# One block's LayerNorm sums on ScalarE, remainder rows used last, fewer zero blocks, another PV order and a three-piece tail in a fused attention and FFN kernel

## Chip, cores and metric

One core of one Trainium2 chip. The metric is the device time of one execution in microseconds; lower is better. A timing is the median of several executions. The kernel before took 562.42 us (three runs, 562.17 to 563.18).

## The reference

```python
def reference(A_x, A_wqkv, A_wo, B_x, B_w_gate, B_w_up, B_w_down):
    x = A_x                                   # [1, 2048, 576] bf16
    xn = _layernorm(x, axis=-1)
    s = _A_ref(xn, A_wqkv, A_wo)              # 32 heads of 18, causal window of 256 keys, softmax, wo
    g = _silu(_B_ref(xn, B_w_gate, B_w_up, B_w_down))   # (sigmoid(xn wg) * (xn wu)) wd, F = 4608
    return x + s * g
```

## The kernel before

The program builds a graph of operations (each one a short list of instructions of one engine), places them on the engines with a list scheduler that uses estimated durations and priorities, and emits one straight instruction stream per engine. Tokens go in four chunks of 512 (four blocks of 128). TensorE works nearly always in pairs of matmuls, one in each 64-row half of the array; "PV" is attention's product of the softmax weights with the values, 16 groups of narrow matmuls (four a chunk) on smaller tiles. The contraction of 576 is cut into 4 x 128 "main rows" (`wgs`) and 64 "remainder rows" (`wgr`); an FFN tile of 128 hidden features is done in a first half (`f10`) and a second half (`f11`), and the remainder pair was the first of the first half:

```python
BLOCKS = (range(KB), range(1, KB))           # k = 0 is the remainder
def turn(eng, outs, lhs, rhs, hi):
    for k in BLOCKS[hi]:
        res = pair(eng, outs, ..., not hi and k == 0, bool(hi) and k == KB - 1, hi)
# gate_up(ft, h, half, ...):
    o = op("PE", len(BLOCKS[half]) * mm_ns(n), f, f"f1{half}:{c}:{ft}", deps=[xin, wops[ft // WG], deps], ...)
```

In the first chunk the normalised x blocks reach TensorE by transposes, so that the first FFN tiles are done in four token parts each; warming matmuls (`NWARM`) fill the time before (in the trace pairs of them start 0.43 us apart up to 3.6 us and 0.22 us apart from 3.9). The weights of a tile pair have four buffers (`NWS`), the remainders of four tiles have two (`NWR = 2`). All these loads are issued by SyncE, one in-order queue, in the scheduler's order:

```python
self.op_wgr[wg] = self.load_rem(self.wgr[:, sr, :], (self.wg[:, f8], self.wu[:, f8]), ..., pr, [dr])
```

The end: the last token block's down projection (2 x 288 columns) was split once, so that 2 x 192 columns could be worked up by ScalarE and VectorE while TensorE did the last 2 x 96 (in the trace from 554.78 to 556.58 us, TensorE's last matmul starting at 556.07); one transfer took the whole block out.

```python
NTAIL = 96
            na = D // 2 - NTAIL
            down(i + 1, hs[1], 1, [la], 0, na, range(NFG - 1))
            lb = down(i + 1, ht, 0, [], 2 * na, NTAIL)
            fa = down(i + 1, hs[1], 1, [la], 0, na, range(NFG - 1, NFG))
            self.build_final(sb + 1, hs[1], fa, 0, na)
            self.build_final(sb + 1, ht, down(i + 1, ht, 1, [lb], 2 * na, NTAIL), 2 * na, NTAIL)
```

The softmax here doesn't subtract the row's maximum and nothing guards it: scores larger than these inputs give would overflow.

## Time and profile before

| | before |
|---|---|
| median of three runs | 562.42 us |
| span of the profiled execution | 560.1 us |
| first useful matmul starts | 7.87 us |
| last matmul starts | 556.07 us |
| from there to the end | 4.05 us |
| TensorE busy | 99% |

### The profile page before, as it was taken

How to read it: one execution, taken by the hardware profiler on the slowest of the kernel's cores; microseconds unless marked ns; L12 is line 12 of the kernel's file. 1: busy time of each engine (PE TensorE's matmuls, PEld its weight loads, DVE VectorE, ACT ScalarE, POOL GpSimd, SP SyncE). 2: the span in 40 equal slices, each digit the busy share in tenths (PEclk: the TensorE clock that was granted, in tenths of full speed). 3: DMA queues.
4: the chain of work that ended last, by engine and by line, in shares of the span. 5: the costliest groups of instructions: out<-in, count | busy, mean ns of one | idle time of the engine just before them, and what ended most of it. 6: DMA issues, size and time to landing. Idle time of an engine off the chain costs nothing.

```text
span 560.1 us, 19180 instructions
## 1 busy us (share of the span) xinstructions
PE 553.5 (99%) x8300; PEld 335.7 (60%) x8300; DVE 335.7 (60%) x793; ACT 271.4 (48%) x379; POOL 210.8 (38%) x358
## 2 busy tenths in 40 slices
PE   8999999999999999999999999999999999999997
PEld 4454544677764454556877566555487754444786
DVE  5576879769587776734886773586656133333133
ACT  3245655545655656466655636665754133323011
POOL 4564467473366534405674530465330100000000
PEclk9999999999999999999999999999999999999999
DMA  8975899541215454427321243454521126552010
GB/s 230 319 216 153 241 279 261 154 59 35 76 37 155 133 143 144 116 75 128 97 58 35 81 116 98 125 157 125 164 66 36 32 70 176 166 161 57 1 44 23
DMA packets 113323, 67.81 MB, mean 121 GB/s; under 512 B 18476, under 2 KB 111372, under 8 KB 113240
## 3 DMA queue, kind: packets, MB, share of 16 engines
q1 hardware_dynamic: 105816, 60.68, 39.6%
q0 software_dynamic: 7424, 5.92, 3.9%
q8 instruction: 65, 1.06, 0.8%
q14 instruction: 18, 0.15, 0.1%
HBM read 55.15 MB, written 2.36 MB: 103 GB/s over the span
## 4 chain that ended last, share of the span: by engine, by line
PE 97%; DVE 2%; DMA 0%; issue 0%; DVEq 0%
PE ps L109 93%; PE ps L754 3%; DMA x<-in_A_x_dram 0%; DVE o2T L780 0%; DVE ot L772 0%; DVE small L503 0%; DVE s_attn L1005 0%; DVE small L505 0%; DVE o L776 0%; DVE thf L1010 0%; DVE v_aug L652 0%; DVE xnr L515 0%; PE ps L553 0%; DVE xf L1015 0%; DVE ot L775 0%
## 5 line engine op out<-in xcount | busy, mean ns | idle before, releaser
L109 PE MATMUL ps<-xnT,wgs 64*128 64x512 bf16 (+1 forms) x2400 | 285.6, 368 | 0.1
L704 ACT ACTIVATE expr<-ps 128x1024 bf16<-128x1024 f32 (+2 forms) x160 | 156.7, 979 | 86.6 <-PE ps L109 86.0
L109 PEld LDWEIGHTS ps<-xnT,wgs 64*128 64x128 bf16 x2400 | 113.8, 94 | 116.8 <-PE ps L109 0.9
L109 PE MATMUL ps<-wd_sb,hT 64*128 64x288 bf16 (+2 forms) x2448 | 154.3, 276 | 0.0
L900 DVE SCALAR_TENSOR_TENSOR hT<-tring,ps 128x512 bf16<-128x512 bf16 x144 | 98.0, 683 | 89.6 <-ACT tring L897 87.1
L897 ACT ACTIVATE tring<-ps 128x512 bf16<-128x512 f32 x144 | 85.9, 597 | 114.4 <-PE ps L109 112.7
L109 PEld LDWEIGHTS ps<-wd_sb,hT 64*128 64x128 bf16 x2448 | 113.1, 94 | 28.0
L265 POOL DMA_DIRECT2D qk<-qd x160 | 82.6, 524 | 106.6 <-PE ps L109 99.8
L717 DVE TENSOR_TENSOR expr<-expr,mask 128x256 bf16<-128x256 bf16 (+2 forms) x232 | 63.7, 305 | 53.2 <-ACT expr L704 52.5
L669 POOL TENSOR_SCALAR kx<-kprev,small 128x256 bf16<-128x256 bf16 x64 | 62.0, 979 | 31.5 <-PE ps L109 30.8
L265 POOL DMA_DIRECT2D oT<-o2T x72 | 36.9, 520 | 61.9 <-DVE o2T L780 50.0
L109 PE MATMUL ps<-qk,kx 64*128 64x320 bf16 (+4 forms) x736 | 59.8, 251 | 0.0
L109 PE MATMUL ps<-xnT,wgr 64*128 64x512 bf16 (+1 forms) x300 | 55.9, 368 | 0.3
L109 PEld LDWEIGHTS ps<-qk,kx 64*128 64x128 bf16 x736 | 32.0, 94 | 25.5 <-DVE hT L900 1.4
L109 PE MATMUL ps<-xnT,wqk 64*128 64x512 bf16 x256 | 32.6, 377 | 0.0
L772 DVE STREAM_TRANSPOSE ot<-ps 128x512 f32<-128x512 f32 x32 | 22.4, 701 | 13.4 <-PE ps L754 13.3
L995 ACT ACTIVATE thf<-ps 128x576 bf16<-128x576 f32 (+3 forms) x22 | 11.4, 519 | 36.3 <-PE ps L109 35.8
L591 DVE CAST qd<-ps 128x1024 bf16<-128x1024 f32 (+1 forms) x20 | 22.2, 1114 | 6.2 <-PE ps L109 5.9
L669 DVE TENSOR_SCALAR kx<-qk,small 128x512 bf16<-128x512 bf16 x64 | 22.2, 373 | 3.3 <-PE ps L109 3.1
L780 DVE STREAM_TRANSPOSE o2T<-o 128x512 bf16<-128x512 bf16 x32 | 22.8, 711 | 1.1
L109 PEld LDWEIGHTS ps<-xnT,wgr 64*128 64x128 bf16 x300 | 15.0, 94 | 13.8 <-issue 1.3
L825 ACT ACTIVATE s_attn<-ps 128x576 bf16<-128x576 f32 x16 | 9.9, 648 | 27.1 <-PE ps L109 27.1
(64 smaller groups left out, 301.9 us busy)
## 6 DMA issues: line engine op xcount, KB each, us to landing
wgs<-in_B_w_gate_dram SPq DMA_DIRECT2D x72, 256.0 KB, 3.4
wgs<-in_B_w_up_dram SPq DMA_DIRECT2D x72, 256.0 KB, 3.9
wd_sb<-in_B_w_down_dram SPq DMA_DIRECT2D x9, 576.0 KB, 6.4
qk<-qd POOLq DMA_DIRECT2D x100, 36.0 KB, 2.3
wgr<-in_B_w_gate_dram SPq DMA_DIRECT2D x36, 64.0 KB, 2.3
wgr<-in_B_w_up_dram SPq DMA_DIRECT2D x36, 64.0 KB, 2.4
xf<-in_A_x_dram SPq DMA_DIRECT2D x16, 144.0 KB, 2.7
out_dram<-xf SPq DMA_DIRECT2D x16, 144.0 KB, 1.8
```

The costliest lines, as they stand in the source:

```text
L109: res = eng.matmul(outs[i], lhs(ROWS[t], i), rhs(ROWS[t], i), start=start, stop=stop, tile_position=(64 * t, 0))
L265: o = self.op(eng, DMA_ISSUE_NS[eng], lambda e: e.dma_start(dst, src), name, deps, prio, nbytes=nbytes)
L591: return eng.tensor_copy(dst, self.both(h, n))
L669: return e.tensor_scalar(self.kx[:, sx, pos:pos + n_ // SW, t, :], src.rearrange("p (s k) -> p s k", k=SW), self.half[:, t:t + 1], None, A ...
L704: return eng.activation(self.expr[:, se, :, lo * SW:NT], self.both(h, NT)[:, :, lo * SW:NT], ACTF.Exp, scale=SM_SCALE)
L717: return eng.tensor_tensor(e_, e_, m_, ALU.mult)
L754: res = eng.matmul(outs[i][p0:p0 + VH, cols], self.v_aug[ROWS[i], o:o + VH], self.expr[ROWS[i], se, t, cols], start=n == 0, stop=n == len( ...
L772: return e.transpose(self.ot1[:, p1, :], self.halves(hp, NT)[i])
L780: t2 = op("DVE", dve_ns(NT), lambda e, p2=p2, p3=p3: e.transpose(self.o2T[:, p3, :], self.o2[:, p2, :]), f"ot2:{c}:{pr}:{i}", deps=[on, d3 ...
L897: th = op("ACT", act_ns(NT), lambda e: e.activation(self.tring[:, st, :], bank(h, 0), ACTF.Tanh, scale=0.5), f"th:{c}:{ft}", deps=[pg, dt_ ...
L900: mu = op("DVE", dve_ns(NT), lambda e: e.scalar_tensor_tensor(self.hT[:, ft, :], self.tring[:, st, :], 1.0, bank(h, 1), ALU.add, ALU.mult) ...
L995: return e.activation(v2(t)[:, a:b, :], y2()[:, a:b, :], ACTF.Tanh, scale=0.25)
```

## The change

Its intent: start TensorE's useful work earlier (the third x block's LayerNorm sums on ScalarE, so that VectorE gets to the fourth sooner; remainders last, so that the first FFN matmul needs fewer weights), leave out 32 score matmuls whose keys don't exist in the first chunk, order the PV blocks narrow first, space the score groups by a table, and end with a smaller last piece (60 and 52 columns after 176) and an early transfer of the big piece. The diff, cut to its core; cuts are marked:

```diff
+PV_ORDER = (-4, 7, -3, 6, -2, 5, -1, 4, 0, 1, 2, 3)      # was (0, 5, -4, -3, -2, -1, 1, 2, 3, 4, 6, 7)
-BINS0 = (((-4, 0, 1), (1, 1, 5), (6, 6, 2)), ((-2, 2, 1), (3, 3, 5)), ((0, 0, 5), (5, 5, 3)), ...
+BINS0 = (((0, 0, 5), (5, 5, 3)), ((1, 1, 5), (6, 6, 2)), ((2, 2, 5), (7, 7, 1)), ((3, 3, 5),), ((4, 4, 4),))
-NTAIL = 96
-NWARM = (11, 4, 1)
+NTAIL = (60, 52)
+REM_PRIO = 0.6
+STATS_ACT = (2,)
+NWARM = (11, 3)
-SPACE_NS = 1500.0
+SPACE_NS = ((1700, 1700, 1700, 1400, 1700, 2200, 900, 1700), ...)      # one per chunk and head group
-BLOCKS = (range(KB), range(1, KB))
+BLOCKS = ((1, 2, 3, 4), (1, 2, 3, 4, 0))
...  # LayerNorm of block 2 of the first chunk
+    def act_stats(self, x_in, o_x, pr):
+        a1 = op("ACT", ..., lambda e: e.activation(junk, x_in, ACTF.Identity, accum_out=sx), ...)
+        m = op("POOL", 150, ...)                      # minus mean
+        a2 = op("ACT", ..., lambda e: e.activation(junk, x_in, ACTF.Square, bias=nm, accum_out=sq), ...)
+        v = op("POOL", 150, ...); rs = op("POOL", 560, ...)   # variance + eps, power -1/2
...  # remainder loads
-                                                ("wgr", sr), pr, [dr])
+                                                ("wgr", sr), pr + REM_PRIO, [dr])
...  # gate_up: the first half waits for main rows alone
-deps=[xin, wops[ft // WG], deps]
+deps=[xin, wops[ft // WG][0:1 + half], deps]
...  # the third tile's first half is placed ahead of the second tile's last second half
...  # tail
+            nb, nc_ = NTAIL
+            lb = down(i + 1, hb, 0, [], 2 * na, nb)
             fa = down(i + 1, hs[1], 1, [la], 0, na, range(NFG - 1, NFG))
             self.build_final(sb + 1, hs[1], fa, 0, na)
+            lc = down(i + 1, hc, 0, [], 2 * (na + nb), nc_)
+            self.build_final(sb + 1, hb, down(i + 1, hb, 1, [lb], 2 * na, nb), 2 * na, nb)
+            self.build_final(sb + 1, hc, down(i + 1, hc, 1, [lc], 2 * (na + nb), nc_), 2 * (na + nb), nc_)
...
-        if c0 + w == D:
+        if c0 == 0 or c0 + w == D:                   # first piece leaves in a transfer of its own
```

## The prediction

> **What bounds the kernel now.** I read the page first, then the chain of work that ended last, then the timelines of the first 15 us and the last 10 us on every engine, and then the spacing of all 8300 matmul starts.
>
> ```profile
> span 560.1 us, 19180 instructions
> PE 553.5 (99%) x8300; PEld 335.7 (60%) x8300; DVE 335.7 (60%) x793; ACT 271.4 (48%) x379; POOL 210.8 (38%) x358
> PE 97%; DVE 2%; DMA 0%; issue 0%; DVEq 0%
> ```
>
> TensorE is busy 99% of the span and makes up 97% of the chain; the next engine stands at 60%. So a saving counts only if it removes TensorE work, starts TensorE's useful work earlier, ends the work behind its last matmul sooner, or fills a hole in TensorE's stream. The spacing shows how little there is. Matmuls run in pairs on two 64-row tiles; a pair of N columns follows the one before after N/2.4 + about 2.7 ns (512 columns: 216 ns; 288 columns: 122 ns). Summing start-to-start intervals gives 555.0 us; N/2.4 alone gives 536.2. The 18.8 us between them: 3.1 in the warm-up matmuls at the start, some 9.2 in the 2.7 ns of each pair, 4.6 around the PV groups, and under 2 us in real waits: 0.84 before 14.3 us, 0.26 at 130.0, 0.28 at 327.3, and 0.06 to 0.12 at three places. The rest of the span is the start (first useful matmul at 7.87 us) and the end.
>
> The start:
>
> ```profile
> 3.08 0.46 DVE L503 BATCH_NORM_STATS2 small<-x 128x6 f32<-128x288 bf16 x1 [2.08 <-DMA x<-in_A_x_dram]
> ...
> 5.87 1.03 PE L109 MATMUL ps<-hT 64*128 64x512 bf16 x8
> ...
> 7.49 0.38 PE L109 MATMUL ps<-hT 64*128 64x512 bf16 x2
> 7.87 0.23 PE L109 MATMUL ps<-xnT,wgr 64*128 64x128 bf16 x2
> ...
> 10.38 0.23 PE L109 MATMUL ps<-xnT,wgr 64*128 64x128 bf16 x2
> ...
> 11.30 0.49 DVE L541 COPY xnT<-ps 128x640 bf16<-128x640 bf16 x1 [0.28 <-PE ps L553]
> 11.85 0.23 PE L109 MATMUL ps<-xnT,wgr 64*128 64x128 bf16 x2
> ...
> 13.10 2.13 PE L109 MATMUL ps<-xnT,wgs 64*128 64x512 bf16 x16
> ```
>
> VectorE normalises four x blocks one after another, 1.6 us each, from 3.08 to 10.49; TensorE transposes each, an engine copies it out, and only then can FFN matmuls of that block run. The first FFN matmul (7.87) reads wgr, the remainder rows, whose DMA landed last of its four weight loads, at 7.74 (gate and up main rows: 6.33 and 7.32). The fourth block's copy ends at 11.80, so TensorE stands still from 11.54 to 11.85.
>
> The end:
>
> ```profile
> 556.32 0.25 ACT L995 ACTIVATE thf<-ps 128x96 bf16<-128x96 f32 x1 [0.81 <-PE ps L109]
> 556.50 0.61 DVE L1005 TENSOR_TENSOR s_attn<-s_attn,ps 128x96 bf16<-128x96 bf16 x2
> 556.78 0.25 ACT L995 ACTIVATE thf<-ps 128x96 bf16<-128x96 f32 x1 [0.22 <-DVE s_attn L1005]
> 557.14 0.36 DVE L1010 SCALAR_TENSOR_TENSOR thf<-thf,s_attn 128x192 bf16<-128x192 bf16 x1
> 557.53 0.26 DVE L1015 TENSOR_TENSOR xf<-xf,thf 128x192 bf16<-128x192 bf16 x1
> ```
>
> From the last matmul (modelled end 556.27) to the last VectorE result (557.79) are 1.5 us, then 2.3 us for the output transfer.
>
> [...]every one of the 16 PV groups (64x32 tiles) is entered 92-93 ns and left 94-95 ns later than the streaming explains, whether the block before was 512, 288 or 64 columns wide. [...]the trace has PV matmuls 8 ns apart just where a narrow block left no time for the loads. [...]The trace's 576-column ACTIVATE takes 648 ns[...].[...]
>
> **Part by part.**
>
> 1. Start. The third block's statistics leave VectorE: two halves (0.37 each spaced), aggregate 0.22, epsilon 0.15 = 1.1 us. ScalarE is free from 2.3 until the first copy at 6.08; the block lands at 4.16, so two passes of about 0.75 (648[...]) fit in 4.2-6.0, with GpSimd's small steps between (its power takes 0.55-0.57). VectorE's last duplicate then falls at about 9.4 or sooner instead of 10.49. TensorE needs from its first FFN matmul: 8 parts of 9 pairs x 56 ns = 4.03, two transposes 0.30. Using remainders last, the first half needs gate and up only: start near 7.45 (7.32 + 0.1), with main rows first for both early tiles, and remainders are there at 7.74. Without a hole 7.45 + 4.35 = 11.8 for the end of the eight parts, where the kernel before has 12.87. Fourth block needed at about 10.7, ready near 10.4: just enough. The 0.23 us between the halves of the third tile (13.76 to 14.20) goes too, as its first half is placed ahead. Ideal 1.07 + 0.23 = 1.3; I take **-1.2**. The next weights allow it: third tile's main rows landed at 9.54 and 10.38, needed at 11; fifth tile's 12.25 and 12.73, needed near 13.8.
> 2. Zero blocks. First chunk, 8 head groups, two 64-column pairs each fall away: 16 x 31.4 ns (the 144 such matmuls average 15.7 ns) = **-0.50**, all on TensorE. ScalarE also loses 128 of 2048 columns per tile of its exps, VectorE gains one mask per head group; both lie beside TensorE.
> 3. PV order. Streaming is unchanged: 40 x 64 columns (30 in the first chunk). Drains stay at 93 + 94. What can change is the narrow blocks. Before, chunks 1-3 take 1277 ns a group, the first chunk's 942; pairs plus exit drain explain 1193 and 914. A 64-column block leaves 27 ns to load eight weights for the next. Before, 64 then 128 sits mid-group and the rest of the group runs 8 ns per tile apart. After, 64, 64, 128, 128 lie together and the first chunk, which had no such place, gets 64, 128. By the observed delays (78 ns for the 64-to-128 step at the last tile, about 60 a round of loads) I get about +24 ns in 12 groups and +54 in 4: **+0.5**; the author presumably measured something better, so I count **+0.3**.
> 4. Score spacing. Per head group instead of 1.5 us everywhere, it moves only the order of work on TensorE. It can win at most the 0.26 + 0.28 and the three small waits, 0.8 in all; I count **-0.3**.
> 5. Tail. Second-to-last pieces: 72 pairs at 76 ns (176 columns, before 192: 82.7) is -0.48; 60 and 52 columns, 72 pairs each at 27.7 and about 25 (near the smallest spacing seen) = 3.8 against 72 x 42.2 = 3.04: +0.75. TensorE +0.3. The chain behind the last matmul shrinks: 52 instead of 96 columns in ScalarE's and VectorE's steps and 104 instead of 192 in the two last, some 0.4 in all, and VectorE no longer finishes the big piece at 556.59 just as the last one arrives. Most of the last block leaves earlier in its own transfer, but the last transfer still has its latency (median 1.8 us)[...]. Together **-0.2**.
>
> Sum: -1.2 - 0.5 + 0.3 - 0.3 - 0.2 = **-1.9 us**, so 562.4 becomes **560.5**. Everything before the tail shifts TensorE's whole stream, since FFN work fills it to the end.
>
> **The rivals.**
> - ScalarE's statistics come in the way: GpSimd has to do the power for blocks 1 and 2 at once (6.04-6.59 is taken), or the second pass delays the copy at 6.08. For: both lie within 0.1 us. Against: the first FFN matmul is held by weights at 7.4 anyway. If the fourth block comes late, the gain shrinks to 0.6: 561.1.
> - Weights become the bound. DMA is 99% busy from 7.8 to 14.3. Then the start gains only 0.45: 561.3. Against: landings run ahead of use by 0.7 us or more from the third tile on.
> - PV's drain on leaving is hidden behind a wide last block[...]. That would be 16 x 94 = 1.5 us: 558.7. Against: entering after a 512-column matmul costs the same 93.
> - The new score spacing opens holes where VectorE or ScalarE has not yet freed a bank: each of the size of the present ones, 0.1-0.3; +0.8 at worst: 561.6.
>
> **Range and chances.** The parts are small and nearly independent: start 0.4, PV 0.5, spacing 0.4, tail 0.2, run-to-run 0.3 (the three runs before span 1.0) give about 0.9 in the root of squares: **559.1 to 561.8**. Two per cent are 11 us; all holes of TensorE together are under 10, and nothing in the change adds more than 1 us of work. Faster by 2%: 0.005; within: 0.99; slower: 0.005.
>
> **What would show it.** Right: first FFN matmul near 7.4 and reading wgs; the third tile done near 13.8 instead of 15.07; 112 instead of 144 score matmuls of 64 columns; PV entered and left at 93-95 ns and 1290-1310 ns long; span 558-559. Wrong: the start unchanged (weights or the fourth block late), PV groups under 1200 ns (drain hidden), or new idle time of TensorE between 14 and 550 us.

Passages that no trace or run shows are cut from it, with the cut marked. The sum is as recorded: -1.2 - 0.5 + 0.3 - 0.3 - 0.2 = -1.9 us, so 560.5. Its tail term, -0.2, is +0.3 of streaming and -0.5 behind the last matmul: -0.4 of steps and -0.1 for a smaller last transfer. That -0.1, which had no measured basis, is among the cuts (from the last VectorE result to the end took 2.32 us before and 2.10 after). So are 0.1 of the 0.75 us a pass, for reading ScalarE's sum; 648 ns were measured. "Drains" are the 92 to 95 ns by which PV groups are entered and left late. Where PV matmuls are 8 ns apart, the weight loads are 8.3 ns apart in the trace before: eight take 66 ns, and a block of 64 columns streams in 27. That PV may start with a 64-column block was not shown before the change; the runs with that order are correct (e1, e9).

## More of the kernel before

The prediction shows the lines of the chain, the start and the end. Three more of the page matter later; they are of its DMA queues (packets, MB, share) and its DMA issues (count, KB each, median us from issue to landing):

```profile
q8 instruction: 65, 1.06, 0.8%
...
wgr<-in_B_w_gate_dram SPq DMA_DIRECT2D x36, 64.0 KB, 2.3
wgr<-in_B_w_up_dram SPq DMA_DIRECT2D x36, 64.0 KB, 2.4
```

Queue 8 brings TensorE's part of the program (the counts of its instructions below fit that): 65 packets of 16384 bytes each.

## The result, and the profile after

| | before | after |
|---|---|---|
| median (six runs each) | 562.52 us (561.79 to 563.18) | 563.60 us (562.89 to 564.47) |
| ratio, 95% interval | | 1.0021 [1.0008, 1.0034] |
| span of the profiled execution | 560.1 | 561.2 |

A ratio here and below is the mean time of one kernel's fast runs over that of the other's of the same rounds, so it is not quite the ratio of the medians quoted. The predicted 560.5 us and its range (559.1 to 561.8) were missed: the kernel is about 1 us slower, within 2%.

The page of the changed kernel:

```profile
span 561.2 us, 19415 instructions
...
PE 554.0 (99%) x8408; PEld 348.5 (62%) x8408; DVE 333.7 (59%) x801; ACT 274.6 (49%) x385; POOL 211.6 (38%) x360
...
q8 instruction: 66, 1.08, 0.8%
...
PE 97%; DVE 1%; DMA 1%; issue 0%; SPq 0%; DVEq 0%
...
wgr<-in_B_w_gate_dram SPq DMA_DIRECT2D x36, 64.0 KB, 3.9
wgr<-in_B_w_up_dram SPq DMA_DIRECT2D x36, 64.0 KB, 3.7
```

TensorE still fills 97% of the chain. Three things differ: 108 more matmuls and as many weight loads, one more packet of program, and remainder loads that land a median of 3.7 and 3.9 us after issue.

The start, TensorE and ScalarE of the changed kernel (start, duration, engine, line, instruction, count, and in brackets the idle time before and what ended it):

```profile
7.54 0.40 PE L120 MATMUL ps<-xnT,wgs 64*128 64x128 bf16 x8 [0.89 <-DMA wgs<-in_B_w_up_dram]
...
12.96 0.22 PE L120 MATMUL ps<-xnT,wgr 64*128 64x128 bf16 x2
13.56 1.04 PE L120 MATMUL ps<-xnT,wgs 64*128 64x512 bf16 x8 [0.38 <-PE ps L120]
```

```profile
4.48 0.68 ACT L584 ACTIVATE tring<-x 128x576 bf16<-128x576 bf16 x1 [2.19 <-DMA x<-in_A_x_dram]
5.07 0.19 ACT L584 ACTIVATION_READ_ACCUMULATOR tring<-x 128x1 f32 x1
```

The parts predicted are there: ScalarE's two passes (0.68 and 0.77 us, each followed by 0.19 us for reading its sum, of which 0.09 lie behind the ACTIVATE's end), a first FFN matmul on main rows at 7.54 us. VectorE's last duplicate ends at 9.74 instead of 10.49, and the fourth block's copy at 10.79 instead of 11.79. But behind the two matmuls of 12.96 TensorE does nothing until 13.56: 0.55 us by the start-to-start interval less the streaming, 0.38 in the view's brackets, which count from the modelled end of the matmul before. The view names a semaphore, but by the code the wait is for the third tile's first half, and the trace has that update of the semaphore at 12.92 (the last one before the hole ends is at 13.19), so the wait must have another reason.

The end of the changed kernel, all engines; and the last steps of its chain of work:

```profile
555.72 3.76 SPq L277 DMA_DIRECT2D out_dram<-xf  x2
556.33 1.50 PE L120 MATMUL ps<-wd_sb,hT 64*128 64x60 bf16 x103 [0.93 <-issue]
...
558.85 0.21 DVE L1071 TENSOR_TENSOR xf<-xf,thf 128x104 bf16<-128x104 bf16 x1
```

```profile
472.41 82.98 PE ps L120 x1241
555.40 0.93 issue
556.33 0.61 PE ps L120 x31
```

The chain says "issue" for 0.93 us: TensorE waits for no semaphore there. The kernel before has no such step. Counted from the start-to-start intervals less the streaming, the hole is 1.09 us.

To see where the time went I split the two executions into the same pieces. "Holes" are the parts of start-to-start intervals that exceed the streaming by more than 40 ns, without the entries and exits of PV:

| us | before | after | difference |
|---|---|---|---|
| first FFN matmul starts | 7.87 | 7.54 | -0.33 |
| holes, start (to 16 us) | 0.84 | 0.55 | -0.29 |
| holes, middle | 0.79 | 2.02 | +1.23 |
| holes, last 16 us | 0.00 | 1.09 | +1.09 |
| columns streamed, at 2.4 a ns | 532.51 | 532.23 | -0.28 |
| entries and exits of PV | 3.00 | 2.99 | -0.01 |
| all smaller intervals | 11.05 | 11.23 | +0.18 |
| behind the start of the last matmul | 4.05 | 3.51 | -0.54 |
| sum | 560.11 | 561.16 | +1.05 |

(The 2.4 columns a ns are read from the spacing, as in the prediction: 216 ns for 512 columns, 122 for 288. In the -0.28 of columns streamed, -0.43 are the zero blocks; +0.13 are one block's transposes, which now stand behind the first FFN matmul.)

Of the +1.23 in the middle, 0.69 are two waits for remainder loads, 0.37 at 74.5 and 0.32 at 471.9. The second, in the weight loads of TensorE:

```profile
472.38 0.57 PEld L120 LDWEIGHTS ps<-xnT,wgs 64*128 64x128 bf16 x8 [0.62 <-DMA wgr<-in_B_w_gate_dram]
```

So there were two suspects, each with a rival. **Theory 1:** the remainder loads wait too long in SyncE's queue because of their lower priority; rival: the memory side got slower. **Theory 2:** the hole in the tail and the one at 12.96 are TensorE waiting for its own program. Queue 8's packets are 16384 bytes each, and the trace fits one packet for every 256 of TensorE's records. I count these from 0 (matmuls, weight loads and its own semaphore waits, 16824 before and 17040 after); the hole at the start stands at record 449, the hole in the tail at record 16833, and 16833 - 449 is 64 x 256. With the boundaries at 193 + 256 n, the blocks from record 449 to the one fetched ahead at the end are 65 and 66, as many as queue 8 has packets. The fetch of the block that begins at record 16833 ran from 553.95 to 554.88, while TensorE ran the block before, which had begun at 553.35; the new block's first matmul started at 556.33, 2.38 us after its fetch began. Rival: a wait of the new tail itself, for a PSUM bank or for ScalarE.

### The profile page after: what moved, and what is told of

The parts are those of the page before. It is cut to its first block, busy times and chain, and to the rows that moved or that the text cites. A ratio compares the mean times of both kernels' runs of the same rounds, so it can differ in the third digit from the quotient of the medians.

```text
span 561.2 us, 19415 instructions
## 1 busy us (share of the span) xinstructions
PE 554.0 (99%) x8408; PEld 348.5 (62%) x8408; DVE 333.7 (59%) x801; ACT 274.6 (49%) x385; POOL 211.6 (38%) x360
## 3 DMA queue, kind: packets, MB, share of 16 engines
q8 instruction: 66, 1.08, 0.8%
## 4 chain that ended last, share of the span: by engine, by line
PE 97%; DVE 1%; DMA 1%; issue 0%; SPq 0%; DVEq 0%
PE ps L120 93%; PE ps L799 3%; DMA wgs<-in_B_w_up_dram 1%; SPq L277 0%; DVE o2T L825 0%; DVE ot L817 0%; DVE o L821 0%; DVE s_attn L1061 0%; DVE v_aug L696 0%; DVE thf L1066 0%; DVE ot L820 0%; PE ps L597 0%; DVE xf L1071 0%; DVEq L1226 0%
## 5 line engine op out<-in xcount | busy, mean ns | idle before, releaser
L749 ACT ACTIVATE expr<-ps 128x1024 bf16<-128x1024 f32 (+4 forms) x160 | 154.9, 969 | 89.3 <-PE ps L120 88.8
L120 PEld LDWEIGHTS ps<-xnT,wgs 64*128 64x128 bf16 x2400 | 118.3, 94 | 111.9 <-issue 3.2
L120 PE MATMUL ps<-wd_sb,hT 64*128 64x288 bf16 (+3 forms) x2592 | 155.7, 269 | 0.9 <-issue 0.9
L120 PEld LDWEIGHTS ps<-wd_sb,hT 64*128 64x128 bf16 x2592 | 119.9, 94 | 22.1 <-issue 1.3
L762 DVE TENSOR_TENSOR expr<-expr,mask 128x128 bf16<-128x128 bf16 (+2 forms) x240 | 63.9, 297 | 78.8 <-ACT expr L749 78.1
L120 PE MATMUL ps<-qk,kx 64*128 64x320 bf16 (+1 forms) x704 | 59.9, 254 | 0.1
L1051 ACT ACTIVATE thf<-ps 128x576 bf16<-128x576 f32 (+4 forms) x24 | 11.7, 489 | 35.0 <-PE ps L120 34.6
L695 ACT ACTIVATE v_aug<-ps 64x288 bf16<-64x288 f32 x32 | 13.1, 408 | 17.0 <-PE ps L120 16.5
```

Source lines behind the costliest of these rows:

```text
L120: res = eng.matmul(outs[i], lhs(ROWS[t], i), rhs(ROWS[t], i), start=start, stop=stop, tile_position=(64 * t, 0))
L695: return eng.activation(dst, src, ACTF.Copy)
L749: return eng.activation(self.expr[:, se, :, lo * SW:NT], self.both(h, NT)[:, :, lo * SW:NT], ACTF.Exp, scale=SM_SCALE)
L762: return eng.tensor_tensor(e_, e_, m_, ALU.mult)
```

## The experiments

Twelve kernels, all correct. Those of one call shared the runs of the kernel before: e1 to e4 (561.79 us, nine runs), e5, e6, e9 and e10 (562.19, eleven), e11 to e14 (562.06, nine). All runs compared were fast; e5 and e6 are single looks, of unknown state, without a ratio ("-"). The holes and spans are those of one profiled execution each.

| run | median us | ratio to before, 95% | span | first FFN matmul | holes start / middle / tail | behind last matmul |
|---|---|---|---|---|---|---|
| after | 563.60 | 1.0021 [1.0008, 1.0034] | 561.16 | 7.54 | 0.55 / 2.02 / 1.09 | 3.51 |
| e1_tail_two | 563.20 | 1.0028 [1.0016, 1.0041] | 562.28 | 7.41 | 0.99 / 2.82 / 0.00 | 4.88 |
| e2_pv_old | 562.95 | 1.0025 [1.0012, 1.0039] | 561.27 | 7.54 | 0.11 / 2.86 / 1.07 | 3.51 |
| e3_rem_prio0 | 564.92 | 1.0053 [1.0040, 1.0065] | 562.81 | 7.14 | 0.63 / 3.43 / 1.19 | 3.51 |
| e4_space_flat | 564.65 | 1.0051 [1.0037, 1.0064] | 562.85 | 7.59 | 0.20 / 3.56 / 1.26 | 3.52 |
| e5_tail_80_80 | 563.22 | - | 561.48 | 8.12 | 0.00 / 2.25 / 1.13 | 3.60 |
| e6_tail_four | 566.10 | - | 564.36 | 8.18 | 0.05 / 2.57 / 3.38 | 3.59 |
| e9_rem_early | 561.86 | 0.9989 [0.9977, 1.0001] | 559.83 | 7.39 | 0.06 / 1.34 / 1.07 | 3.52 |
| e10_tail_before | 562.70 | 1.0005 [0.9987, 1.0023] | 560.80 | 7.33 | 0.18 / 3.09 / 0.00 | 4.04 |
| e11_three_mends | 560.96 | 0.9978 [0.9965, 0.9990] | 559.17 | 7.46 | 0.39 / 1.35 / 0.00 | 4.04 |
| e12_three_warm | 560.69 | 0.9973 [0.9961, 0.9986] | 558.95 | 7.57 | 0.08 / 1.36 / 0.00 | 4.03 |
| e13_only_tail | 565.45 | 1.0057 [1.0043, 1.0070] | 564.79 | 8.62 | 1.01 / 0.79 / 3.24 | 3.42 |
| e14_mends_flat | 563.07 | 1.0018 [1.0006, 1.0031] | 561.41 | 7.38 | 0.28 / 3.60 / 0.00 | 4.04 |

**Parts undone, one at a time (e1 to e4).**

e1: the tail in two pieces, the early first transfer kept.

```diff
-NTAIL = (60, 52)
+NTAIL = (96,)          # tail code generalised to a list of narrow pieces
```

> The changed kernel with its last token block in two pieces (192 and 96 columns a half) again, the early first transfer kept; everything before the tail is in the same order. Theory (the 1.09 us hole at 555.21, which waits for no semaphore, is TensorE running out of fetched instructions because 52- and 60-column pairs use four instructions in 25 to 28 ns): the hole is gone, TensorE streams 0.28 us less, the chain behind the last matmul is 0.4 to 0.5 longer, so 0.8 to 1.0 us faster than the changed kernel, about 562.7. Rival (the hole is chance or has to do with the place in the program, and the three pieces gain what I predicted): a hole stays, or the time is 0.2 us longer than that of the changed kernel.

The hole in the tail is gone, with 16752 TensorE records in the stream. The time did not fall, as the end took 4.88 us behind the last matmul: SyncE issued the first output transfer at 557.94 and the last only at 560.31, though VectorE's last result was there at 559.12. The trace shows what SyncE did in between: 31 waits, one for each lane of loads, which the program puts just ahead of SyncE's last entry (`run_engine`); they take from 558.34 to 560.21. In the kernel after, where the first issue is at 555.72, they are over at 558.00 and the last transfer follows its result at once; in the kernel before they are over at 554.88. As the code stands, the early transfer thus only suits a tail in which some 2.3 us lie between the two, an estimate from these two traces (557.94 to 560.21 and 555.72 to 558.00); moving the waits ahead of it was not run. e10 below removes both.

e2: the old order of PV.

```diff
-PV_ORDER = (-4, 7, -3, 6, -2, 5, -1, 4, 0, 1, 2, 3)
+PV_ORDER = (0, 5, -4, -3, -2, -1, 1, 2, 3, 4, 6, 7)
```

> The changed kernel with the old order of the PV blocks, all else in the same order. Theory from the traces (narrow blocks together load weights slower than they stream): the 12 groups of chunks 1 to 3 go from 1302 back to 1277 ns, the 4 of the first chunk stay at 941, so 0.3 us faster, about 563.3. Rival (the new order helps whoever waits for PV): no change or slower.

PV groups of chunks 1 to 3 fall from 1302 to 1277 ns, those of the first chunk stay at 941 to 942; all are entered within 93 ns and left within 94 to 96. The new order costs 0.30 us (12 groups of 25 ns), nothing in the first chunk. In the kernel after, the weight loads behind the narrow blocks are 8.3 ns apart, as in the kernel before. The span did not show it, as the waits for remainder loads came out larger in this execution (1.08 and 0.43).

e3: the remainder loads' priority back to that of before.

```diff
-REM_PRIO = 0.6
+REM_PRIO = 0.0
```

> The changed kernel with the remainder rows' loads issued at their group's own priority again, remainder rows still used last. Theory (the later issue of those loads makes TensorE wait for them at 74.45 and 471.88, 0.37 and 0.32 us): both waits go, the remainder loads' median from issue to landing goes from 3.8 back to below 3, 0.4 to 0.7 us faster, about 563.0. Rival (the waits come from DMA traffic moved by the new score spacing): waits for weights of the same size stay.

A miss as an experiment. The waits at 74.45 and 471.88 are gone and the loads' median from issue to landing is 2.1 and 2.3 us, as theory 1 says; but TensorE waits 0.53 us for a remainder load in another place (81.5; issued at 76.64, landed at 82.12), the middle has 3.43 us of holes and the time is the longest of the four. The scheduler had made another order of all of TensorE's work out of the one number. So one priority can't be changed alone here; e9 changes the order of SyncE's queue and nothing else.

e4: all score groups at 1.5 us again.

```diff
-SPACE_NS = ((1700, 1700, 1700, 1400, 1700, 2200, 900, 1700), ...)
+SPACE_NS = ((1500,) * 8,) * 4
```

> The changed kernel with 1.5 us between score tiles everywhere, as before. Theory (the table of spacings makes the small waits of TensorE in the middle: 2.03 us in 12 places against 0.79 in 5 in the kernel before): they fall to 1 us or less, 0.6 to 1.2 us faster, about 562.7. Rival (they come from the remainder loads and from the new order of halves): 0.3 us or less of change.

The middle gets worse, 3.56 us of holes. My theory that the table makes the new holes in the middle fell. As in e3, the scheduler makes another order of the work, from TensorE's 568th matmul on, so what is compared is two whole plans.

**The tail (e5, e6, e10, e13).**

e5: two narrow pieces of 80 columns; e6: three of 60, 60 and 52.

```diff
-NTAIL = (60, 52)
+NTAIL = (80, 80)          # e5
+NTAIL = (60, 60, 52)      # e6
```

> The changed kernel with three pieces in the tail of 128, 80 and 80 columns a half in place of 176, 60 and 52. A pair of 80 columns takes 36 ns, so 256 instructions last 2.3 us instead of 1.7. Theory (a fetch of instructions takes some 2.4 us from its start to use, so the stream starves only where 256 instructions are used up sooner): the hole in the tail shrinks to 0.3 us or less. Rival (the third piece itself, its bank or its transfer makes the hole): about 1.1 us again.

> The changed kernel with four pieces in the tail of 116, 60, 60 and 52 columns a half: 288 more narrow instructions. Theory (instruction supply): a second hole of about 1 us follows some 256 instructions after the first, 2 us of holes in all. Rival (one hole belongs to one place in the program or to the end of the three pieces): one hole, 1.1 us.

TensorE at the end of e6:

```profile
555.63 1.85 PE L120 MATMUL ps<-wd_sb,hT 64*128 64x60 bf16 x128 [1.31 <-issue]
559.22 1.73 PE L120 MATMUL ps<-wd_sb,hT 64*128 64x60 bf16 x119 [1.75 <-issue]
```

e6 puts a second hole exactly 256 records behind the first (16833 and 17089), 128 matmuls apart as the count in the first line says; counted from the intervals they are 1.48 and 1.91 us. I had expected 2 us in all and got 3.38. e5 has its hole of 1.13 us at record 16833 although the block before it lasted 2.38 us; I had expected 0.3 or less. Place and number are as theory 2 says; the size was not. Over the runs with a hole in the tail, the fetch begins 0.5 to 0.8 us after TensorE has entered the block before (1.1 to 1.2 at the second boundary of e6 and e13), and the new block's instructions run 2.3 to 3.2 us after the fetch began; the two sum to 3.0 to 3.9 us, not 2.3, which such a block would have to last. It is no fixed limit: one block earlier in e6, 256 records pass in 2.51 us without a hole, as the fetch had begun 0.51 us before TensorE entered that block. What sets the moment at which a fetch begins stays open.

e10: tail and output of the kernel before, whole.

```diff
-NTAIL = (60, 52)
+NTAIL = 96               # and the tail and output code of before, one last transfer
```

> The changed kernel with the tail exactly as before: two pieces, one last transfer. The first trial of this kept the early transfer, and the 1.2 us by which its last transfer was issued late took back what the missing hole gave. Theory (the hole of 1.1 to 1.3 us in the three-piece tail is the instruction supply): no hole after 545 us, 4.05 us from last matmul start to the end (3.51 in the changed kernel), streaming 0.28 less: 0.8 to 1.0 us faster than the changed kernel, ratio about 1.0005. Rival (three pieces gain): ratio 1.0025 or above.

No hole in the tail, and 4.04 us behind the last matmul as in the kernel before. The ratio's interval is wide and overlaps that of the kernel after, so the times alone don't show the gain; its middle still holds three waits for remainder loads (0.46, 0.59, 0.70).

e13: the kernel before with the three-piece tail alone, its order unchanged ahead of it.

```diff
-NTAIL = 96
+NTAIL = (60, 52)          # and the tail and output code of after
```

> The kernel before with the three-piece tail alone; everything ahead of the tail is in the same order. Theory of the instruction supply: the added 288 TensorE records carry the stream past the boundary at record 16833, so a hole of about 1.1 us stands there; with +0.3 us of narrower streaming and -0.54 us behind the last matmul the sum is +0.8 us, ratio about 1.0015. Rival, the tail term of my prediction: no hole, -0.2 us, ratio 0.9997.

TensorE at the end of e13:

```profile
557.43 2.69 PE L109 MATMUL ps<-wd_sb,hT 64*128 64x60 bf16 x128 [1.83 <-issue]
561.17 0.41 PE L109 MATMUL ps<-wd_sb,hT 64*128 64x52 bf16 x11 [1.05 <-issue]
```

Two holes, at records 16833 and 17089, again 128 matmuls apart. I had expected one: 16824 + 288 = 17112 crosses both boundaries, which I had overlooked. From the intervals they are 1.99 and 1.25 us, 3.24 in all, in a profiled execution that was the slowest of the five (566.53; the median is 3.4 us above the kernel before). It also started late, when its first remainder load landed, and its granted clock fell to 0.5 at 558.07, after the first hole and with work left: what it streamed in the tail took 0.9 us more than in the kernel after. No other trace here has that fall before its last matmul. The tail of the change by itself makes the kernel before 0.57% slower; the prediction's -0.2 us is refuted. The rival, a wait of the tail itself, is refuted too: the same tail has one hole in 17040 records and two in 17112.

**The remainder loads (e9).** Only SyncE's list is edited: after scheduling, each remainder load goes ahead of the first entry that starts after its buffer is free.

```diff
+        for o in [o for o in prog["SP"] if o.name.startswith("dma:wgr") and o.deps]:
+            ready = max(d.end for d in o.deps)
+            # move o to just before the first SP entry whose scheduled start is >= ready
```

> The changed kernel with only the order of the sync engine's DMA issues altered: each remainder-row load goes out as soon as its buffer is free, ahead of the attention output moves it stood behind; TensorE, VectorE, ScalarE and GpSimd keep the changed kernel's order. Theory (standing behind those moves costs the waits for remainder rows at 74 and 472 us, 0.4 to 1.1 us each in the four traces so far): no remainder wait after the start, smallest lead of a remainder load over its use above 1 us, 0.7 to 1.5 us faster than the changed kernel, ratio to the kernel before 1.000 or below. Rival (the waits come from a busy DMA system and return elsewhere): waits for weights of the same sum, ratio 1.002.

SyncE around the first wait, in the kernel before, the changed kernel and e9 (start, time to issue, transfer, count):

```profile
64.01 1.24 SPq L265 DMA_DIRECT2D wgr<-in_B_w_up_dram  x1
65.29 3.17 SPq L265 DMA_DIRECT2D oT<-o2T  x4
```

```profile
65.14 3.17 SPq L277 DMA_DIRECT2D oT<-o2T  x4
68.36 0.52 SPq L277 DMA_DIRECT2D wgr<-in_B_w_gate_dram  x1
...
70.11 0.53 SPq L277 DMA_DIRECT2D wgr<-in_B_w_up_dram  x1
```

```profile
63.97 0.60 SPq L277 DMA_DIRECT2D wgr<-in_B_w_gate_dram  x1
...
66.04 3.17 SPq L277 DMA_DIRECT2D oT<-o2T  x4
```

The buffer is free at about 63.1 to 63.3 in before and after. Before issues its loads at once; after, they stand behind four moves of the attention output and are issued 5 and 7 us later, and the second lands at 74.83 where TensorE wants it at 74.45. In e9 they are ahead of the moves again, after the start every load is there 2 us or more before its use, no wait for one is left, and the median from issue to landing is back at 2.3 and 2.1 us: the longer 3.7 to 3.9 was met only while they were issued late. Theory 1 holds; the rival, slower memory, doesn't. The middle's holes fall to 1.34 us, and the ratio to 0.9989. Of the 1.33 us by which this span is shorter than that of the kernel after, 0.68 are the holes in the middle; most of the rest is the start, which e9 did not change (no hole at record 449 in this execution).

**All mends together (e11, e12, e14).** e11 joins e9, e10 and e2; e12 also takes away three pairs of warming matmuls; e14 is e11 with the flat spacing.

```diff
-NWARM = (11, 3)
+NWARM = (11, 0)                    # e12, on top of e11
-SPACE_NS = ((1700, ...), ...)
+SPACE_NS = ((1500,) * 8,) * 4      # e14, on top of e11
```

> The changed kernel with its three losses mended at once: the tail of the kernel before (two pieces, one last transfer), the remainder loads given to the sync engine's queue as soon as their buffer is free, and the old PV order. My theory: the loss of the change is the sum of a 1.09 us tail hole, some 0.7 us of waits for remainder loads and 0.27 us of PV, less what it gains at the start and in the zero blocks. Then this run has no wait for a remainder load, no hole in the tail, PV groups of 1277 ns, a span of 558.7 to 559.3 us and a ratio to the kernel before of 0.997 to 0.998. Rival: the gain comes back as other holes in the middle whatever is mended; ratio 0.999 or more.

> The run with the three mends, with 11 warming matmuls fewer-by-number ahead of the first block boundary (twelve TensorE instructions fewer). Theory: the hole at the first boundary comes because its fetch starts late; with fewer instructions ahead of it the boundary falls later in the work and the hole shrinks, a gain of 0 to 0.4 us against the run with the three mends. Rival: [...]the time is the same or up to 1 us longer.

> The run with the three mends, with every score group of every chunk spaced at 1.5 us in place of the table. From the two earlier runs (holes in the middle 1.3 us with the table and early remainders, 3.6 us without the table) I expect about 2 us more than the run with the three mends, all of it as holes in the middle. Rival: the table is worth what I predicted, 0.3 us or less.

e11 does all that was expected: no wait for a remainder load, no hole in the tail, PV at 1277 ns, span 559.17, ratio 0.9978. What the change gains is thus real, and about 1.2 us; what it lost lay in the three parts mended. e12 moves record 449 twelve instructions further into the work. TensorE at the start of e12:

```profile
13.04 0.22 PE L120 MATMUL ps<-xnT,wgr 64*128 64x128 bf16 x2
13.10 1.03 PE L120 MATMUL ps<-xnT,wgs 64*128 64x512 bf16 x8
```

The hole between these two groups, 0.55 us in the kernel after and 0.14 in e11, is gone. That doesn't show that the shift removed it: e2, e3, e5, e6 and e9 have none there either, without a shift. The span is 0.22 us shorter than e11's and the median 0.27, but the intervals overlap, so a gain over e11 is not shown. e12 has the lowest median, ahead of the kernel before by 0.3% and of the kernel after by 0.5% (0.9973 and 1.0021 of the kernel before, measured in different calls).

e14 loses 2.1 us of median against e11, and its middle holes grow from 1.35 to 3.60 us. As with e4, the whole plan differs. The changed kernel needs its table; 0.3 us, the rival and my prediction, was far too little for it. It does not say that the table helps the kernel before: that was not run.

## Why the prediction was wrong

By its own steps, in us, measured between the profiled executions of before and after:

| step | predicted | measured |
|---|---|---|
| start, up to the end of the third tile | -1.2 | -0.42 (next tile starts at 14.65, was 15.07) |
| zero blocks | -0.5 | -0.43 streamed, and about -0.08 of pair spacing |
| PV order | +0.3 | +0.30 |
| score spacing | -0.3 | other holes in the middle +0.54; not shown to be the spacing's |
| smaller intervals elsewhere | not in the sum | -0.38 (what is left; no run explains it) |
| waits for remainder loads | not in the sum | +0.69 |
| tail, streaming of more pairs | +0.3 | +0.28 |
| tail, behind the last matmul | -0.5 | -0.54 |
| tail, program not there in time | not in the sum | +1.09 |

**Right.** The zero blocks (144 score matmuls of 64 columns became 112), PV's sum and its 93 and 95 ns of entry and exit, and both terms of the tail that I had worked out. PV was right in sum only, and by luck: +24 a group came out as +25 in the twelve groups, but the first chunk's +54 came out as 0, and the +0.3 was a guess below the +0.5 that had been worked out. The rival that ScalarE's second pass delays the first copy came true (6.38 instead of 6.08) and cost nothing, as it said: TensorE waited for weights until 7.54.

**Wrong, the tail.** "Together -0.2" took TensorE's streaming and the chain behind it as the whole cost of 288 more instructions. What failed is that they have to be supplied: the new tail passes 256 records in 1.86 us where, in the runs with a hole, 0.5 to 0.8 us went by until the next fetch began and 2.3 to 3.2 more until its instructions ran. TensorE stood still for 1.09 us. e1, e6, e10 and e13 show it, with holes only where the stream passes a boundary in narrow pairs, and as many holes as boundaries. The kernel before has 16824 records, nine fewer than lie ahead of number 16833.

**Wrong, the start.** "Without a hole 7.45 + 4.35 = 11.8" and "just enough" named the inputs rightly: the weights and the fourth block came in time. Of the 0.78 us that are missing, the profiled execution lost 0.55 at record 449, whose fetch began late, at 10.97, 2.2 us after the block before was entered, with the DMA engines 99% busy (7.8 to 11.0 us). About 0.1 is the start at 7.54 instead of 7.45, as the weights landed a little later, and about 0.15 fits a block's transposes: three now stand behind the first FFN matmul (7.76, 8.40, 9.91), where the sum has two. The loss depends on the execution: none in e9, where that fetch began at 10.32 and the next tile started at 14.01, 1.06 us earlier than before, which is near the predicted 1.2; 0.55 in after; 0.99 in e1, fetch at 11.31. In e13, which has the kernel before's order, a hole of 0.17 stands at the same record, at 13.84 (fetch at 11.82). That the busy DMA engines delay this fetch is an inference; no run changed their load. It fits that of the eight fetches of the kernel after that began over 1.5 us after TensorE's entry, seven had a DMA share of 0.84 or more in the 1.5 us before.

**Wrong, a rival not seen.** The list of rivals has a weight that becomes the bound only for the start. The part "remainders last" was counted as a gain there; that a lower priority puts 72 loads behind others in an in-order queue for the whole kernel was not worked out. It costs 0.69 us in the profiled execution (e9 removes it), and 0.9 to 1.8 in the five other traces with the same order of SyncE's loads (e1, e2, e5, e6, e10).

**Wrong in size, the spacing.** It "can win at most ... 0.8" held for the holes of the kernel before. In the changed kernel the plan with the flat spacing has 2.2 us more of them (e14), so the table is a repair and not a gain. About 0.5 us of new holes remain in the middle, e.g. 0.23 at 23.1 and 0.24 at 40.5, the latter waiting for keys from VectorE. They are in e11 and e12 as well, and no run took them away: their cause stays open.

## What to carry to other kernels

When a change adds small instructions to the busiest engine, count how many instructions pass per microsecond, not only their durations: here stretches of 256 records that ran in 1.7 to 2.5 us waited for their own program, and one of 2.5 us did not. How long such a stretch has to last is estimated at 3 to 4 us, from the two parts that summed to 3.0 to 3.9 us in the runs with a hole. The profile calls that wait "issue" (0.93 us at 555.40) or puts it down to a semaphore that came before (at 12.92, for the hole up to 13.56). A lower priority for a load that shares an in-order queue must be followed to every place where that queue blocks, not only where the change was meant to act (here two waits of 0.69 us together). And before a narrower last piece is chosen, look at what else it adds: here the gain of 0.5 us behind the last matmul cost 1.1 to 3.4 us in front of it.
